# Dividing the exponentials of one block size on GpSimd instead of ScalarE, in a fused attention and two-layer expert kernel

## The chip, the cores and the metric

The kernel runs on one core of one Trainium2 chip. The metric is the time of one execution on the device in microseconds; for the kernel before there are three timed runs and one profiled execution.

## The reference, cut

Attention over 4 batches of 8 heads with 576 positions of 64 numbers, with a causal mask and a decay that comes from a running sum of log(f); then two dense layers over all 2304 tokens: one takes the largest of three products, the other puts a rational function between two products.

```
scores = scale * np.matmul(q, k.transpose(0, 1, 3, 2))
cum = np.cumsum(np.log(np.clip(f, 0.0001, 1.0)), axis=-1)
scores = np.where(causal, -1e9, scores + cum[..., :, None] - cum[..., None, :])
attn = np.exp(scores - max(scores))
attn = attn / (sum(attn) + 1e-09)          # the division that the change moves
x = np.matmul(attn, v)                      # heads side by side: 2304 x 512
h = np.maximum(np.maximum(x @ w1, x @ w2), x @ w3);  x = h @ w_out
h = x @ w_in;  out = (P(h) / (Q(h) + 1e-06)) @ w_out2
```

## The kernel before

Heads are worked on in pairs. A pair's 576 queries are split into two groups: the first has three blocks of queries (with 64, 192 and 320 keys each, by the causal mask), the second has two blocks of 128 queries, one with 448 and one with 576 keys. One head's group is a unit. In the first batch all four pairs' first groups come first (pairs 0 to 3), and then their second groups (pairs 4 to 7), so that the first dense layer can begin on the first group's columns while the second groups are still at the attention. In the three later batches a pair does both groups.

A unit goes through these steps. `scores` (L386 for the first six pairs, L388 and L389 for the others) puts queries times keys into one of two score banks in PSUM; VectorE's L390 reads the bank, adds the mask, keeps the smallest negative score and writes a block `e` to SBUF, which frees the bank; ScalarE's L396 takes exponentials and sums them. `normalise` adds a tiny number to the sums (L401, ScalarE), takes reciprocals (L402, VectorE) and multiplies each block by them: on ScalarE (L406) in the first batch's second group, on GpSimd (L408) elsewhere. `turn` transposes the blocks on TensorE (L428), and ScalarE copies them to `pt` (L430); `attend` multiplies by v (L444), and ScalarE and VectorE split the result into a high part (L451) and a low part (L452), which are `x`.

The dense layer's products in this part of the program are `h` (L476 to L478, twelve matmuls for one tile). A tile is compared with the running maximum `m` by VectorE (L484), which frees one of two banks; the products' outputs `x2p` (L502 to L504) go through L507 (ScalarE) and L508 (VectorE) to `xo`. The first `h` tile of the first batch begins with the low part of `x` of pair 3.

Beside that, weights are prepared throughout this stretch: each piece goes through L181 (ScalarE, size), L186, L187, L188 and L191 (VectorE, bit work in SBUF), L197 (ScalarE, high part) and L200 (GpSimd, low part). Keys and queries of a pair are split by L312 and L324 (ScalarE), L313 and L325 (VectorE), L314 and L328 (GpSimd).

The order of each engine's instructions is not written out by hand here: the program is recorded in steps, and a scheduler that estimates times orders it before the kernel is built. Moving one instruction to another engine therefore moves others too. Each engine then takes its instructions in that order.

Of the kernel before, what the change touches and what calls it, by code (L numbers as in the profile page):

```python
# [37 lines left out]
def kernel(  # L38
# [317 lines left out]
    class Unit:  # L356
# [41 lines left out]
        def normalise(self):  # L398
            blks = GBLK[self.g]
            n = len(blks)  # L400
            nc.scalar.activation(self.rs[:, 0, :n], self.rs[:, 0, :n], AF.Identity, bias=tiny)  # L401
            nc.vector.reciprocal(self.rs[:, 1, :n], self.rs[:, 0, :n])  # L402
            for j, i in enumerate(blks):
                e = self.e[i]
                if self.pair.b == 0 and self.g == 1:
                    nc.scalar.activation(e, e, AF.Copy, scale=self.rs[:, 1, j : j + 1])  # L406
                else:
                    nc.gpsimd.tensor_scalar(e, e, self.rs[:, 1, j : j + 1], 0.0, op0=ALU.mult, op1=ALU.add)  # L408
# [450 lines left out]
```

## Time and profile before

| what | value |
|---|---|
| median of 3 runs (lowest to highest) | 954.58 us (954.29 to 955.71) |
| profiled execution: its time | 954.83 us |
| profiled execution: its span | 953.0 us |
| TensorE busy | 932.1 us (98%) |
| VectorE busy | 723.2 us (76%) |
| ScalarE busy | 649.0 us (68%) |
| GpSimd busy | 239.7 us (25%) |

The span is the time between the first and the last instruction on the core; the profiled execution's own time has 1.8 us more around it. TensorE is busy almost throughout, so the other engines' shares say little by themselves: what counts are the few microseconds in which TensorE waits, and stretches in which its clock is at the lower of two levels.

### The profile page before, as it was taken

The numbers are of one execution on the slowest core, as the hardware profiler recorded it, in microseconds if no ns is written. First come the engines' busy times: TensorE is split into PE (matmuls) and PEld (weight loads), VectorE is DVE, ScalarE is ACT, GpSimd is POOL, SyncE is SP. The second block draws the span as 40 slices with busy tenths as digits, with TensorE's granted clock in tenths as the row PEclk, the third lists the DMA queues.
The fourth block names the chain that finished last, engine by engine and source line by source line (L and its number), as shares of the span: only waits on it lengthen the run. The fifth ranks groups of instructions, "written<-read, shape, count | busy, mean of one in ns | idle before, by whom it ended". The sixth has DMA issues, their size and how long they took to land.

```text
span 953.0 us, 16820 instructions
## 1 busy us (share of the span) xinstructions
PE 932.1 (98%) x5780; PEld 825.9 (87%) x5780; DVE 723.2 (76%) x1692; ACT 649.0 (68%) x1542; POOL 239.7 (25%) x392
## 2 busy tenths in 40 slices
PE   6999999999999999999999999999999999999998
PEld 4768899988999999999999988888888888899997
DVE  8578865556777776524397969888988988899996
ACT  6798777777777677546354567667666666777765
POOL 4344444444555455414132400000000000000000
PEclk9988999999999999999999999999999999999999
DMA  7864332123555564220245386011002102100000
GB/s 192 218 191 119 98 84 58 44 77 107 154 148 167 153 174 140 75 78 2 72 140 188 122 300 231 1 45 45 0 1 67 45 1 67 44 1 1 34 1 34
DMA packets 125743, 88.53 MB, mean 93 GB/s; under 512 B 74573, under 2 KB 110425, under 8 KB 125657
## 3 DMA queue, kind: packets, MB, share of 16 engines
q1 hardware_dynamic: 125656, 87.45, 30.6%
q8 instruction: 46, 0.75, 0.3%
q14 instruction: 41, 0.33, 0.1%
HBM read 64.73 MB, written 22.69 MB: 92 GB/s over the span
## 4 chain that ended last, share of the span: by engine, by line
PE 79%; DVE 12%; ACT 5%; issue 2%; DMA 2%; SPq 0%; ACTq 0%; DVEq 0%
PE hq L734 7%; PE oo L782 7%; PE oo L783 7%; PE hq L732 7%; PE hq L733 7%; PE oo L781 7%; PE h L476 5%; PE h L477 5%; PE h L478 5%; PE tp L428 5%; PE o L444 5%; PE s L388 2%; PE s L389 2%; PE x2p L502 2%; PE x2p L504 2%
## 5 line engine op out<-in xcount | busy, mean ns | idle before, releaser
L476 PE MATMUL h<-x,w1h 128*128 128x320 f32 (+1 forms) x576 | 175.4, 305 | 2.1 <-DVE x L452 1.3
L477 PE MATMUL h<-x,w1h 128*128 128x320 f32 (+1 forms) x576 | 171.8, 298 | 0.0
L478 PE MATMUL h<-x,w1l 128*128 128x320 f32 (+1 forms) x576 | 171.3, 298 | 0.0
L476 PEld LDWEIGHTS h<-x,w1h 128*128 128x128 f32 x576 | 109.3, 190 | 4.0 <-DVE m L484 1.9
L782 PE MATMUL oo<-wp,gh 128*128 128x512 f32 x288 | 112.6, 391 | 0.0
L781 PE MATMUL oo<-wp,gh 128*128 128x512 f32 x288 | 112.0, 389 | 0.0
L741 ACT ACTIVATE s<-hq 128x512 f32<-128x512 f32 (+1 forms) x80 | 44.3, 554 | 97.3 <-PE hq L734 97.2
L477 PEld LDWEIGHTS h<-x,w1h 128*128 128x128 f32 x576 | 109.3, 190 | 0.7 <-issue 0.5
L478 PEld LDWEIGHTS h<-x,w1l 128*128 128x128 f32 x576 | 109.1, 190 | 0.2 <-issue 0.2
L783 PE MATMUL oo<-wp,gl 128*128 128x512 f32 x288 | 109.1, 391 | 0.0
L396 ACT ACTIVATE e<-e,st 128x64 f32<-128x64 f32 (+4 forms) x160 | 88.9, 557 | 28.9 <-DVE st L390 26.5
L408 POOL TENSOR_SCALAR e<-e,rs 128x64 f32<-128x64 f32 (+4 forms) x144 | 76.2, 545 | 80.7 <-DVE rs L402 71.0
L390 DVE CUSTOM_DVE_ANT_0 e<-s,mask 128x320 f32<-128x320 f32 (+3 forms) x160 | 67.2, 432 | 32.4 <-PE s L389 21.2
L430 ACT ACTIVATE pt<-tp 128x384 f32<-128x384 f32 (+3 forms) x160 | 70.3, 469 | 15.3 <-PE tp L428 14.2
L744 DVE SCALAR_TENSOR_TENSOR s<-s,ab,u 128x512 f32<-128x512 f32 (+1 forms) x80 | 55.7, 697 | 32.2 <-ACT u L742 32.0
L428 PE MATMUL tp<-ident,e 128*128 128x128 f32 (+1 forms) x480 | 77.0, 279 | 0.0
L734 PE MATMUL hq<-x,wil 128*128 128x512 f32 (+1 forms) x192 | 69.8, 364 | 0.0
L732 PE MATMUL hq<-x,wih 128*128 128x512 f32 (+1 forms) x192 | 69.8, 363 | 0.0
L733 PE MATMUL hq<-x,wih 128*128 128x512 f32 (+1 forms) x192 | 69.6, 363 | 0.0
L783 PEld LDWEIGHTS oo<-wp,gl 128*128 128x128 f32 x288 | 54.1, 188 | 11.3
L782 PEld LDWEIGHTS oo<-wp,gh 128*128 128x128 f32 x288 | 54.0, 188 | 10.6
L781 PEld LDWEIGHTS oo<-wp,gh 128*128 128x128 f32 x288 | 54.1, 188 | 10.4
(133 smaller groups left out, 2433.7 us busy)
## 6 DMA issues: line engine op xcount, KB each, us to landing
raw_w<-in_moe_w_dram SPq DMA_DIRECT2D x18, 512.0 KB
raw_wp<-in_moe_w_out_dram SPq DMA_DIRECT2D x32, 256.0 KB
wpd<-wp SPq DMA_DIRECT2D x32, 256.0 KB
raw_wi<-in_moe_w_in_dram SPq DMA_DIRECT2D x32, 256.0 KB
wp<-wpd SPq DMA_DIRECT2D x10, 768.0 KB
x2d<-xo SPq DMA_DIRECT2D x16, 320.0 KB
out_dram<-ob SPq DMA_DIRECT2D x18, 256.0 KB
kn<-in_k_dram SPq DMA_DIRECT2D x32, 128.0 KB
```

Source lines behind the costliest of these rows:

```text
L396: nc.scalar.activation(e[:nr], e[:nr], AF.Exp, bias=m, scale=-1.0, accum_out=l)
L408: nc.gpsimd.tensor_scalar(e, e, self.rs[:, 1, j : j + 1], 0.0, op0=ALU.mult, op1=ALU.add)
L428: nc.tensor.transpose(tp[:kr, dst : dst + P], self.e[i][:, Q0[c] : Q1[c]], ident)
L476: nc.tensor.matmul(hp_[:, :w], wh[:, j, dc], xs[dc][:, 1], start=(dc == NDC - 1), stop=False)
L477: nc.tensor.matmul(hp_[:, :w], wh[:, j, dc], xs[dc][:, 0], start=False, stop=False)
L478: nc.tensor.matmul(hp_[:, :w], wl[:, j, dc], xs[dc][:, 0], start=False, stop=(dc == 0))
L732: nc.tensor.matmul(hp_[:, :w], wih[:, dc, fs], xh, start=(dc == 0), stop=False)
L733: nc.tensor.matmul(hp_[:, :w], wih[:, dc, fs], xl, start=False, stop=False)
L734: nc.tensor.matmul(hp_[:, :w], wil[:, dc, fs], xh, start=False, stop=(dc == NDC - 1))
L781: nc.tensor.matmul(o, g[0][:, ts_], wh_, start=(fc == 0), stop=False)
L782: nc.tensor.matmul(o, g[0][:, ts_], wl_, start=False, stop=False)
L783: nc.tensor.matmul(o, g[1][:, ts_], wh_, start=False, stop=(fc == NF2 - 1))
```

## The change

In the first batch's second group, the block with 448 keys (`j` is 0) is divided by GpSimd, and only the block with 576 keys (`j` is 1) stays on ScalarE.

```
             for j, i in enumerate(blks):
                 e = self.e[i]
-                if self.pair.b == 0 and self.g == 1:
+                if self.pair.b == 0 and (self.g, j) == (1, 1):
                     nc.scalar.activation(e, e, AF.Copy, scale=self.rs[:, 1, j : j + 1])
                 else:
                     nc.gpsimd.tensor_scalar(e, e, self.rs[:, 1, j : j + 1], 0.0, op0=ALU.mult, op1=ALU.add)
```

Eight units have such a block, so eight instructions change engine, and the scheduler makes another order between the first of them and the end of the first batch's attention. In the names below, the first number behind `e`, `s` and `tp` (4 to 7) or the first pair of numbers is the pair and the head, `rs` the sums and reciprocals of a unit, `cv_w` a weight piece in work, `w1l` its low part; the last number is the tile's own.

GpSimd, from the low part of the weight pieces 3 on, before:

```order
L200 TENSOR_TENSOR w1l_739<-cv_w_3_740,w1h_738 128x512
L200 TENSOR_TENSOR w1l_739<-cv_w_3_757,w1h_738 128x512
L200 TENSOR_TENSOR w1l_739<-cv_w_3_783,w1h_738 128x512
L200 TENSOR_TENSOR w1l_821<-cv_w_4_822,w1h_820 128x512
L200 TENSOR_TENSOR w1l_821<-cv_w_4_845,w1h_820 128x512
L200 TENSOR_TENSOR w1l_821<-cv_w_4_884,w1h_820 128x512
```

and after:

```order
L200 TENSOR_TENSOR w1l_739<-cv_w_3_740,w1h_738 128x512
L408 TENSOR_SCALAR e_4_0_1_813<-e_4_0_1_813,rs_0_1_812 128x448
L200 TENSOR_TENSOR w1l_739<-cv_w_3_757,w1h_738 128x512
L200 TENSOR_TENSOR w1l_739<-cv_w_3_783,w1h_738 128x512
L408 TENSOR_SCALAR e_4_1_1_918<-e_4_1_1_918,rs_1_1_917 128x448
L200 TENSOR_TENSOR w1l_821<-cv_w_4_822,w1h_820 128x512
L408 TENSOR_SCALAR e_5_0_1_1021<-e_5_0_1_1021,rs_0_1_1020 128x448
L200 TENSOR_TENSOR w1l_821<-cv_w_4_845,w1h_820 128x512
L408 TENSOR_SCALAR e_5_1_1_1141<-e_5_1_1_1141,rs_1_1_1140 128x448
```

The divisions of pairs 4 and 5 are queued between the low parts of the weight pieces.

VectorE, where pair 3's `x` is split (`x_1_0_873`, L452) and the scores of pair 5's second head are drained (L390):

```order
 L191 SCALAR_TENSOR_TENSOR cv_w_4_822<-raw_w_4_755,cv_w_4_822 128x512
 L188 SCALAR_TENSOR_TENSOR cv_w_4_845<-raw_w_4_781,cv_w_4_845 128x512
+L390 ISA e_5_1_1_1141,st_1_1_1139<-s_0_5_1_1_1142,mask 128x448
+L390 ISA st_1_1_1139 128x1
 L191 SCALAR_TENSOR_TENSOR cv_w_4_845<-raw_w_4_781,cv_w_4_845 128x512
 L452 TENSOR_TENSOR x_1_0_873<-o_1_0_864,x_1_0_873 128x320
-L390 ISA e_5_1_1_1141,st_1_1_1139<-s_0_5_1_1_1142,mask 128x448
```

The drain of the 448 scores now stands in front of the last bit operation on a weight piece and of the split of `x`.

TensorE, at the first tile of the dense layer (`h_0_0_0_892`), which follows the transposes of pair 4's second head:

```order
 L428 MATMUL tp_4_1_1_992<-ident,e_4_1_1_935 128x128 x2
 L428 MATMUL tp_4_1_1_997<-ident,e_4_1_1_935 64x128
+L386 MATMUL s_1_5_1_1_1160<-kf_119,qf_123 128x256
 L476 MATMUL h_0_0_0_892<-x_1_0_873,w1h_173 128x320
 L477 MATMUL h_0_0_0_892<-x_1_0_873,w1h_173 128x320
```

The last scores of pair 5 now stand in front of the first `h`; before, they stood two tiles later. Further on, the scores of pair 7's first head move from in front of the `h` tile 1915 to behind it, and on ScalarE L406 on 128x448 is gone from all eight units. On SyncE only one load of keys and one store of `x2d` change places.

## Rows read from the trace of the kernel before

**Rows 1.** Page, busy time of each engine over the span.

```profile
PE 932.1 (98%) x5780; PEld 825.9 (87%) x5780; DVE 723.2 (76%) x1692; ACT 649.0 (68%) x1542; POOL 239.7 (25%) x392
```

**Rows 2.** Busy time by stretch: stretch, length, each engine's busy time, granted clock, DMA.

```profile
60.00:66.40 6.40, 4.58 (x24) 2.11 (x23) 6.40 (x15) 6.30 (x17) 2.81 (x3) 1.00 0.61 189
...
66.40:76.70 10.30, 9.80 (x30) 6.60 (x31) 9.88 (x23) 9.89 (x22) 3.35 (x3) 0.50 0.70 222
...
76.70:80.10 3.40, 3.40 (x24) 3.25 (x23) 1.29 (x4) 3.40 (x10) 1.76 (x2) 1.00 0.01 2
...
77.00:146.00 69.00, 67.09 (x482) 60.69 (x482) 54.63 (x149) 54.39 (x145) 33.66 (x47) 1.00 0.34 90
```

**Rows 3.** TensorE in order of time: start, length, operation [idle before, releaser].

```profile
72.71 1.44 PE L386 MATMUL s<-kf,qf 66*128 66x320 f32 x2 [0.44 <-DVE st L390]
73.94 2.13 PE L428 MATMUL tp<-ident,e 128*128 128x128 f32 x9
75.72 0.62 PE L476 MATMUL h<-x,w1h 128*128 128x320 f32 x1
...
79.76 0.60 PE L386 MATMUL s<-kf,qf 66*128 66x256 f32 x2
```

**Rows 4.** VectorE in order of time, same columns.

```profile
66.14 0.41 DVE L187 TENSOR_SCALAR cv_w<-cv_w 128x512 int32<-128x512 int32 x1
66.59 1.64 DVE L188 SCALAR_TENSOR_TENSOR cv_w<-raw_w,cv_w 128x512 int32<-128x512 int32 x1
68.27 0.69 DVE L191 SCALAR_TENSOR_TENSOR cv_w<-raw_w,cv_w 128x512 int32<-128x512 int32 x1
...
70.17 1.09 DVE L187 TENSOR_SCALAR cv_w<-cv_w 128x512 int32<-128x512 int32 x1
...
71.51 0.15 DVE L402 RECIPROCAL rs<-rs 128x2 f32<-128x2 f32 x1
...
74.84 0.48 DVE L452 TENSOR_TENSOR x<-o,x 128x320 fp32r<-128x320 f32 x1
75.25 0.62 DVE L390 CUSTOM_DVE_ANT_0 e<-s,mask 128x448 f32<-128x448 f32 x1
```

**Rows 5.** GpSimd in order of time, same columns.

```profile
66.19 1.50 POOL L200 TENSOR_TENSOR w1l<-cv_w,w1h 128x512 fp32r<-128x512 f32 x1 [0.71 <-ACT w1h L197]
69.70 1.27 POOL L200 TENSOR_TENSOR w1l<-cv_w,w1h 128x512 fp32r<-128x512 f32 x1 [2.02 <-ACT w1h L197]
75.91 2.55 POOL L200 TENSOR_TENSOR w1l<-cv_w,w1h 128x512 fp32r<-128x512 f32 x2 [4.94 <-ACT w1h L197]
```

**Rows 6.** Groups by shape (GpSimd 150 to 480 us, ScalarE 60 to 146): busy, mean ns.

```profile
L408 POOL TENSOR_SCALAR e<-e,rs 128x448 f32<-128x448 f32 x24 | 15.8, 657 | 21.1 <-DVE rs L402 16.3 <-ACT hh L488 2.6 <-DVE st L390 1.4
...
L406 ACT ACTIVATE e<-e,rs 128x448 f32<-128x448 f32 x8 | 5.3, 667 | 0.3 <-DVE rs L402 0.2
```

**Rows 7.** ScalarE in order of time.

```profile
66.01 1.33 ACT L406 ACTIVATE e<-e,rs 128x448 f32<-128x448 f32 x2
...
72.90 1.34 ACT L406 ACTIVATE e<-e,rs 128x448 f32<-128x448 f32 x2
...
75.22 1.14 ACT L197 ACTIVATE w1h<-cv_w 128x512 fp32r<-128x512 f32 x2
...
131.64 0.67 ACT L406 ACTIVATE e<-e,rs 128x448 f32<-128x448 f32 x1 [0.23 <-DVE rs L402]
...
134.00 0.74 ACT L507 ACTIVATE xo<-x2p 128x320 fp32r<-128x320 f32 x2
```

**Rows 8.** TensorE's waits, 77 to 147 us: in total, times, longest.

```profile
PE h L476 <- DVE m L484: 0.8, 3, 0.4
PE s L388 <- DVE q1s L325: 0.4, 1, 0.4
PE x2p L502 <- DVE xo L508: 0.3, 1, 0.3
PE s L388 <- DVE st L390: 0.2, 1, 0.2
```

More of the change, by code (lines that the diff above doesn't have):

```diff
@@ L404, in normalise @@
                 e = self.e[i]
-                if self.pair.b == 0 and self.g == 1:
+                if self.pair.b == 0 and (self.g, j) == (1, 1):
                     nc.scalar.activation(e, e, AF.Copy, scale=self.rs[:, 1, j : j + 1])
```

## The prediction, made before the changed kernel was run

> **What bounds the kernel now.** I read the page first, then the busy time by stretches, then each engine in time order from 62 to 80 us, and last the waits of TensorE behind that. The page has TensorE (PE) busy for 932.1 of 953.0 us [rows 1], so a gain must come out of the 21 us in which it stands still, or out of time in which it runs at the lower clock. An engine beside it that is merely relieved gives nothing. The instructions that the change moves lie between 66 and about 135 us; behind that every engine's order is as before; what the stretch from 66 to 146 us gains or loses is handed on one for one.
>
> In that stretch there are two regimes. From 66.4 to 76.7 us the granted clock is 0.50 throughout, that is 1.2 GHz, against 1.00 in the 3.4 us behind it [rows 2]. TensorE was busy for 4.58 of the 6.40 us ahead of the fall [rows 2], and it has only scores (L386) and transposes (L428) during it, until the dense h products start at 75.72 [rows 3]. VectorE (DVE) and ScalarE (ACT) are busy for 9.88 and 9.89 of these 10.3 us [rows 2]. Here TensorE's pace hangs on VectorE: a score bank is free only once L390 has drained it. The row at 72.71 shows it, 0.44 us idle released by L390 [rows 3]. VectorE fills the time between drains with the bit work on the expert weights (L186 to L191). From 77 us on there is so much product work that TensorE stands still for only 69.00 - 67.09 = 1.91 us up to 146 [rows 2], in short waits, all listed ones for VectorE [rows 8].
>
> **The parts of the change.** *The division itself.* The first batch has eight second-group units. Each loses one ScalarE instruction on 128x448, 667 ns, and gains a GpSimd one on the same block, 657 ns [rows 6]. Eight times 0.667 are 5.3 us off ScalarE. The two blocks of a unit were divided one behind the other, 1.33 us for the pair [rows 7]; they can now run side by side, so the transposes of either may be ready some 0.6 us sooner. No transpose is listed as waiting for ScalarE here [rows 3, 8], so the 0.6 us are worth nothing by themselves.
>
> *What the GpSimd instruction does to VectorE.* The trace shows a price on the other side. L187 on 128x512 takes 0.41 us alone at 66.14, but 1.09 us at 70.17, where it began while GpSimd's L200 (69.70 to 70.97) was running [rows 4, 5]. L188 at 66.59 takes 1.64 us, and ends 0.54 us behind the L200 that began at 66.19 and ended at 67.69, whereas the like-shaped L191 at 68.27 takes 0.69 [rows 4, 5]. So bit work that starts inside a GpSimd instruction waits for its end. Until now GpSimd had nothing but L200 here. The Trainium skill says the same more sharply (SBUF — State Buffer, "Who interferes with whom"): the port pair that the two engines share is locked for a whole instruction, and the second one blocks fully; by that rule the new divisions can only cost VectorE time, and the time saved on ScalarE doesn't offset it.
>
> *66 to 77 us, step by step.* (a) The first division needs the same reciprocal as the ScalarE pair that starts at 66.01 [rows 7]; it begins there or a little sooner and lasts 0.66 us, to about 66.5. L187 at 66.14 then starts inside it, and ends some 0.3 us late. L200, L188 and L191 move by the same 0.3 and don't add to it. Bounds: 0 (it slips into the L390 ahead) and 0.66. (b) The second division comes right behind the reciprocal at 71.51 [rows 4], in front of L186 and L188. Bounds 0 and 0.66; I take the middle, 0.35, since it depends on which of them starts first. (c) The L200 that was at 75.91, beside the drains [rows 5], now starts about half a microsecond sooner, since ScalarE reaches the L197 ahead of it (75.22, [rows 7]) without the division of 0.67 us at 72.90. Its 1.3 us then lie on L191, which is now behind a drain (the order above). Bounds 0 and 0.96, the most that a bit operation was held up (1.64 - 0.68); I take 0.5. (d) The drain of 0.62 us at 75.25 now stands ahead of the subtraction L452, which makes the low half of x that the first h product reads: 0.62 us, certain. L452 ended at 74.84 + 0.48 = 75.32. In sum it ends at 75.32 + 0.3 + 0.35 + 0.5 + 0.62 = 77.1 us, and h starts there and not at 75.72: 1.4 us late. Of this 0.6 us are no loss, because the scores that ran at 79.76 for 0.60 us [rows 3] now run in front of h. Net **+0.8 us**.
>
> The low end: with no hold-up L452 ends at 75.94 and h starts behind the scores moved forward, at 76.3: no loss. Below nothing: the h products that ran at half clock from 75.72 to 76.68 would run at full clock if the clock rises as before and they come later, 0.5 us at best. So -0.5. The high end: 0.66 + 0.66 + 0.96 + 0.62 on 75.32 are 78.2, less 75.72 and 0.6: +1.9.
>
> *77 to 146 us.* The other six divisions lie beside dense products. Two of TensorE's waits should go. One of 0.4 us for q1s [rows 8]: the scores of unit 7 now stand behind twelve more products (some 2 us). One of 0.3 us for xo [rows 8]: ScalarE reaches L507 at 134.0 without the division at 131.64 (0.67, [rows 7]). Against that, six GpSimd instructions of 0.66 us can hold up bit work ahead of L484, which frees the h banks; these waits are 0.8 us in three [rows 8]. Six times half of 0.66 would be 2 us of VectorE, which is busy for 54.63 of the 69.00 us [rows 2], so most of it goes into its idle time; I take 0.2. Together **-0.5 us**. Bounds: -1.9, when all waits of the stretch vanish; upwards 2 us, when all of that VectorE time reaches TensorE.
>
> GpSimd's other work (L200, L490, L314, L328) changes places among itself by a few rows at most, and no DMA is added. SyncE's swap of a key load with a store of x2d has no waiter among TensorE's waits, so nothing.
>
> **Sum.** The profiled execution took 954.83 us, 953.0 of span and 1.8 around it; the median of the three runs is 954.58, 0.25 below. 954.83 + 0.8 - 0.5 = 955.1, and against the median 954.9. I say **955.0 us**. About 0.2% (1.9 us) is what a measurement of this kernel tells from no change, so this counts as no change.
>
> **Rivals.** *The low clock lasts longer (slower).* In before, h had been running for 0.96 us when the clock rose at 76.7; in after it starts at about 77.1, and the time ahead of it holds only the sparse scores and transposes that went on at half clock from 66.4 on [rows 2, 3]. If the rise needs the dense products, it slips with them. Another stretch as long as the one from 76.7 to 80.1 (3.4 us, dense, [rows 2]) at half clock does half its work: +1.7 us on top of the +0.3, 956.8. A slip by just the 1.4 us of h's lateness costs 0.7: 955.8. It decides by whether h has begun by 76.7: lateness above 1 us, so the bounds above straddle it. For it: at 0.50 the trace shows nothing but sparse work until h. Against it: only 0.5 us of idle time are in the whole stretch [rows 2], and VectorE's hold-ups may be at their low ends. The Trainium skill (TensorE: Matmul & The Clock Gate, "What's actually happening") states that the lower rate is the default and that activity releases it; by that rule the rise follows h, and the trace agrees as far as one rise shows it. Chance 0.27.
>
> *ScalarE was the true limit (faster).* It is busy for 9.89 of 10.3 us [rows 2] and gets 1.3 us less to do there; if VectorE's row of work was held by ScalarE's pace, TensorE's waits in 66.4 to 76.7 (0.50) and 77 to 146 (1.91) [rows 2] go together: 954.83 - 2.4 = 952.4. Against it: VectorE's rows show no idle time from 66 to 75.8 [rows 4], and the waits name VectorE [rows 8]. Chance 0.12.
>
> *GpSimd's queue (slower).* A division can stand behind an L200 that waits for ScalarE's L197, and the transposes behind the division. L200 takes 1.3 us [rows 5]; two such waits that reach TensorE are 2.6 us, 957.7. Against it: the L200 ahead of the second division ended at 70.97 [rows 5], before the reciprocal at 71.51 [rows 4] that the division needs as well. Chance 0.06.
>
> That the change does nothing is excluded: ScalarE's order has eight rows fewer and GpSimd's eight more.
>
> **How the numbers follow.** Forecast 0.55, long low clock 0.27, ScalarE 0.12, GpSimd's queue 0.06. The forecast's own bounds are -0.5 to +1.9 and -1.9 to +2 about 954.6, mostly inside 953.4 to 956.4. The range takes in the long low clock at 956.8 with some lateness on top, and leaves out the far ends of the ScalarE and queue cases: 953.2 to 957.3. Faster by over 0.2% (below 952.7) needs nearly the whole ScalarE case: 0.11. Slower by over 0.2% (above 956.5) is the long low clock, the queue, and none of the 0.7 us slip: 0.29. Same: 0.60.
>
> **What would show it.** In the profile after: L187 and L188 near 66 to 68 us and the bit work near 72 us longer where a GpSimd L408 overlaps them; L452 of the first x at 76.5 to 77.7 and h right behind it; the clock at 0.50 again from 66.4, its end either at 76.7 (forecast) or some 3 us later (rival). In 77 to 146 the wait for xo gone, and TensorE idle for 1.2 to 2 us. I am wrong if h starts before 76.3, if the half clock is shorter than 10 us, or if a transpose is seen waiting for GpSimd.

## The result, and the profile after

The changed kernel takes 960.35 us (median of six runs, 959.30 to 961.21), the kernel before 955.47 us in the runs beside it: ratio 1.0052, 95% interval 1.0040 to 1.0063. That is 4.9 us slower, beyond the 0.2% that can be told from no change, and outside the range of 953.2 to 957.3.

The profiled execution took 960.80 us, 5.97 above that of before. The page's row of busy times, beside [rows 1]:

```profile
PE 936.2 (98%) x5780; PEld 828.8 (86%) x5780; DVE 726.6 (76%) x1692; ACT 646.1 (67%) x1534; POOL 245.0 (26%) x400
```

ScalarE is busy for 2.9 us less, GpSimd for 5.3 more. TensorE is busy for 4.1 us longer with the same instructions, so part of the loss is slower work and not waiting. Stretches of TensorE (stretch, length, busy, granted clock, DMA share, GB/s), which answer to [rows 2]:

```profile
65.40:82.50 17.10, 15.66 (x46) 0.50 0.51 158
...
77.00:146.00 69.00, 65.70 (x446) 0.96 0.30 80
...
125.00:151.00 26.00, 24.04 (x178) 1.00 0.32 86
```

The half clock lasts 17.1 us and not 10.3. From 77 to 146 us TensorE stands still for 3.3 us and not 1.9. TensorE in order of time, beside [rows 3] (start, length, operation [idle before, releaser]):

```profile
73.34 0.69 PE L428 MATMUL tp<-ident,e 128*128 128x128 f32 x2 [0.46 <-POOL e L408]
...
74.89 1.70 PE L428 MATMUL tp<-ident,e 128*64 128x128 f32 x7
76.57 1.22 PE L386 MATMUL s<-kf,qf 66*128 66x256 f32 x2
78.23 0.63 PE L476 MATMUL h<-x,w1h 128*128 128x320 f32 x1 [0.44 <-DVE x L452]
...
82.40 0.36 PE L476 MATMUL h<-x,w1h 128*128 128x320 f32 x1
```

A transpose waits 0.46 us for a GpSimd division, and the first h product starts at 78.23, 2.5 us later than in before. VectorE and GpSimd say why, beside [rows 4, 5]:

```profile
66.46 0.71 DVE L187 TENSOR_SCALAR cv_w<-cv_w 128x512 int32<-128x512 int32 x1
...
71.86 0.40 DVE L186 TENSOR_SCALAR cv_w<-cv_w 128x512 f32<-128x512 f32 x1
72.19 0.68 DVE L188 SCALAR_TENSOR_TENSOR cv_w<-raw_w,cv_w 128x512 int32<-128x512 int32 x1
...
74.13 0.68 DVE L188 SCALAR_TENSOR_TENSOR cv_w<-raw_w,cv_w 128x512 int32<-128x512 int32 x1
75.89 0.62 DVE L390 CUSTOM_DVE_ANT_0 e<-s,mask 128x448 f32<-128x448 f32 x1 [1.08 <-PE tp L428]
...
76.44 1.34 DVE L191 SCALAR_TENSOR_TENSOR cv_w<-raw_w,cv_w 128x512 int32<-128x512 int32 x1
77.70 0.48 DVE L452 TENSOR_TENSOR x<-o,x 128x320 fp32r<-128x320 f32 x1
```

```profile
66.25 0.64 POOL L408 TENSOR_SCALAR e<-e,rs 128x448 f32<-128x448 f32 x1 [0.46 <-DVE rs L402]
...
72.04 1.25 POOL L408 TENSOR_SCALAR e<-e,rs 128x448 f32<-128x448 f32 x1 [0.46 <-DVE rs L402]
75.96 1.27 POOL L200 TENSOR_TENSOR w1l<-cv_w,w1h 128x512 fp32r<-128x512 f32 x1 [2.67 <-ACT w1h L197]
```

The drain at 75.89 is the one that the new order put ahead of L452. It stood idle for 1.08 us until transposes had ended. It fills block 3 of pair 5, head 1, and that block lies in the buffer of block 3 of pair 4, head 1, which those transposes were still reading. L191 and L452 queue behind it. In before they stood ahead of the drain and filled that time. Less the shift of 0.31 us explained below, L452 starts 2.55 us later than in before: 0.30 come from the stretched L187 at 66.46, 1.08 from the drain's wait, 0.55 from the drain itself and 0.65 from L191, which runs beside the L200 at 75.96.

Where the 5.97 us arise can be read by the start of like instructions in both traces. At the last attend of pair 3 (61 us, order still common) the changed run is already 0.31 us late, in work that the change doesn't touch. That shift is taken off in what follows. At a product of pair 4's attend (L444, 81.41 us in before) it is 3.26 us late, at pair 9's first key transpose (151.05 us in before) 5.11. From there on it is handed on nearly one for one: 5.7 at the first product of the last stage (L732, 553.9 us in before).

So there are two places. **First, 66 to 82 us: 3.26.** h starts 2.20 us late (77.92 less shift, against 75.72), 0.60 of it regained by the scores moved ahead: 1.6. And h then runs at half clock from 78.23 to 82.4, 4.2 us, where before it did so for 1.0 us: half of the 3.2 us, 1.6. **Second, 82 to 151 us: 1.85**. Between the two points TensorE stands still for 3.1 us and not 1.9; the other 0.7 us lie in time that counts as busy. All listed waits of TensorE from 77 to 147 us (in total, times, longest), beside [rows 8]:

```profile
PE tk L335 <- ACT pt L430: 1.1, 2, 0.8
PE x2p L502 <- DVE xo L508: 1.0, 1, 1.0
PE x2p L502 <- ACT wo L197: 0.5, 1, 0.5
PE h L476 <- DVE x L452: 0.4, 1, 0.4
```

### The profile page after: what moved, and what is told of

It is laid out like the page before. It is cut to its first block, busy times and chain, and to the rows that moved or that the text cites. A ratio compares the mean times of both kernels' runs of the same rounds, so it can differ in the third digit from the quotient of the medians.

```text
span 959.0 us, 16831 instructions
## 1 busy us (share of the span) xinstructions
PE 936.2 (98%) x5780; PEld 828.8 (86%) x5780; DVE 726.6 (76%) x1692; ACT 646.1 (67%) x1534; POOL 245.0 (26%) x400
## 4 chain that ended last, share of the span: by engine, by line
PE 85%; DVE 7%; ACT 3%; issue 2%; DMA 2%; SPq 1%; POOL 0%; ACTq 0%; DVEq 0%
PE hq L734 7%; PE hq L732 7%; PE oo L783 7%; PE oo L782 7%; PE hq L733 7%; PE h L476 7%; PE oo L781 7%; PE h L477 7%; PE h L478 7%; PE o L444 5%; PE tp L428 5%; PE s L388 2%; PE s L389 2%; PE x2p L502 2%; PE x2p L504 2%; PE x2p L503 2%
## 5 line engine op out<-in xcount | busy, mean ns | idle before, releaser
L408 POOL TENSOR_SCALAR e<-e,rs 128x64 f32<-128x64 f32 (+4 forms) x152 | 82.8, 560 | 90.4 <-DVE rs L402 78.2
L390 DVE CUSTOM_DVE_ANT_0 e<-s,mask 128x320 f32<-128x320 f32 (+3 forms) x160 | 67.1, 431 | 33.5 <-PE s L389 21.0
L430 ACT ACTIVATE pt<-tp 128x384 f32<-128x384 f32 (+3 forms) x160 | 69.8, 469 | 13.7 <-PE tp L428 12.7
L732 PE MATMUL hq<-x,wih 128*128 128x512 f32 (+1 forms) x192 | 69.8, 363 | 0.0
L484 DVE TENSOR_TENSOR m<-m,h 128x320 f32<-128x320 f32 (+1 forms) x96 | 43.1, 449 | 26.7 <-PE h L478 14.1
L782 PEld LDWEIGHTS oo<-wp,gh 128*128 128x128 f32 x288 | 54.0, 188 | 10.5
```

The lines of the kernel that those rows point to most:

```text
L732: nc.tensor.matmul(hp_[:, :w], wih[:, dc, fs], xh, start=(dc == 0), stop=False)
L782: nc.tensor.matmul(o, g[0][:, ts_], wl_, start=False, stop=False)
```

## Experiments

Each kernel was timed against the kernel before on the same chip. The table is read as above: start of the first h less the shift at 61 us, length of the half-clock spell around it, lateness against before at the two points, and the ratio of the times.

| run | first h | half clock, us | late at 81 us | late at 151 us | ratio (95% interval) |
|---|---|---|---|---|---|
| before | 75.72 | 10.3 | 0 | 0 | 1 |
| changed | 77.92 | 17.1 | 3.26 | 5.11 | 1.0052 (1.0040 to 1.0063) |
| e1 | 77.94 | 17.1 | 3.48 | 3.93 | 1.0044 (1.0031 to 1.0058) |
| e2 | 75.78 | 13.7 | 1.20 | 1.10 | 1.0013 (1.0001 to 1.0024) |
| e3 | 77.38 | 13.7 | 2.34 | 4.66 | 1.0051 (1.0031 to 1.0071) |
| e4 | 75.74 | 10.2 | 0.46 | 0.38 | 0.9997 (0.9987 to 1.0008) |
| e5 | 75.94 | 10.2 | -0.02 | 3.47 | 1.0031 (1.0017 to 1.0046) |
| e6 | 75.72 | 6.8 | 0.27 | 6.97 | 1.0078 (1.0051 to 1.0104) |
| e7 | 75.72 | 10.3 | 0.53 | 0.57 | 1.0005 (0.9996 to 1.0015) |
| e8 | 77.93 | 10.2 | 1.36 | 3.16 | 1.0041 (1.0026 to 1.0057) |
| e9 | 76.58 | 10.3 | 0.58 | 4.25 | 1.0042 (1.0027 to 1.0057) |
| e10 | 75.89 | 3.4 | -0.26 | -0.09 | 1.0026 (1.0014 to 1.0037) |
| e11 | 75.88 | 10.3 | -0.42 | 4.29 | 1.0039 (1.0026 to 1.0052) |
| e12 | 76.17 | 10.3 | -0.98 | 4.70 | 1.0048 (1.0033 to 1.0063) |
| e13 | 77.94 | 17.0 | 3.63 | 5.12 | 1.0052 (1.0033 to 1.0072) |
| e14 | 75.51 | 6.9 | 4.59 | 1.27 | 1.0020 (1.0008 to 1.0032) |

In e5, e6, e11 and e12 the last scores of pair 5 (0.6 us) come only behind the first point, and in e11 and e12 some h products too, so their lateness there looks too favourable. In e14, 24 h products that stood behind the first point come ahead of it, and in e9 eleven that stood behind the second come ahead of that; there part of the lateness is moved work. e1 and e13, whose order up to 82 us is that of the changed kernel, have its long half clock as well (17.1 and 17.0 us), so it isn't one execution's.

The median has what one trace doesn't: runs of one kernel differ. Among the 23 runs of before beside e1 to e4, the eleven with a mean clock of 0.995 took 954.39 to 957.41 us and the four at 0.991 and 0.989 took 956.94 to 958.16, but the eight between them 953.61 to 957.14, so the mean clock goes with only part of that spread. The runs of the changed kernel have 0.989 to 0.993.

### One place or two: e1, e2

e1 keeps the GpSimd division in pairs 4 and 5 alone, e2 in pairs 5, 6 and 7:

```diff
-                if self.pair.b == 0 and (self.g, j) == (1, 1):
+                if self.pair.b == 0 and self.g == 1 and (j == 1 or self.pair.n in (6, 7)):      # e1
+                if self.pair.b == 0 and self.g == 1 and (j == 1 or self.pair.n not in (5, 6, 7)):  # e2
```

> Only the four units of pairs 4 and 5 divide their 448-key block on GpSimd; the units of pairs 6 and 7 divide it on ScalarE as before. Every engine's order is that of the changed kernel up to about 130 us. Theory (two places of loss: the late first h with the long low clock, and hold-ups at 112 to 146 us): h starts near 78 us, the low clock ends near 82.5, and the loss of the second place (2 to 2.5 us) is gone: before + 3.2, about 958.5. Rival A (only the first place counts, the loss behind 112 us is its echo): before + 5.5, about 960.5. Rival B (only the later divisions cost, the first delay is made good): before + 0 to 0.5.

> The units of pairs 5, 6 and 7 divide on GpSimd, the two of pair 4 on ScalarE as before. With that VectorE's order from 66 to 78 us is that of before, L452 ahead of the drain. Theory of two places: the first h starts within 0.5 us of before's 75.7, the low clock ends near 76.7, and only the loss at 112 to 146 us stays: before + 2 to 2.5, about 957.5. Rival A (one place): before + 0 to 0.5, about 955.5. Rival B (only the later divisions cost): before + 5, about 960.

Measured: e1 959.96 us, e2 957.00, before 956.03. e1 has all of the first place (3.48) and is 3.9 us slower; from 82 to 151 us, without the late divisions, it loses only 0.45. e2, with six of the eight divisions and L452 ahead of the drain as in before, starts h on time. The first place makes most of the loss, and it goes with pair 4. Two things in e2 fit none of the three. It keeps four divisions from 82 to 151 us and loses nothing there (1.20 to 1.10), so the second place isn't a price per division. And its clock stayed at half for 13.7 us, 3.6 of them behind the start of h, though h started on time once its shift at 61 us (2.36) is taken off; that alone is its 1.2 us at the first point (TensorE in order of time, then the half-clock stretch):

```profile
78.14 0.61 PE L476 MATMUL h<-x,w1h 128*128 128x320 f32 x1
```

```profile
68.00:81.70 13.70, 12.62 (x39) 0.50 0.58 185
```

### Which division of pair 4: e3, e4

Both leave one more division on ScalarE: e3 that of pair 4, head 1 (near 72 us), e4 that of head 0 (near 66 us); the lists go on with all units of pairs 5 to 7.

```diff
-                if self.pair.b == 0 and (self.g, j) == (1, 1):
+                if self.pair.b == 0 and self.g == 1 and (j == 1 or (self.pair.n, self.h) not in [(4, 0), (5, 0), ...]):  # e3
+                if self.pair.b == 0 and self.g == 1 and (j == 1 or (self.pair.n, self.h) not in [(4, 1), (5, 0), ...]):  # e4
```

> As the changed kernel, but head 1 of pair 4 divides on ScalarE: no GpSimd division beside VectorE's bit work at 72 us. The drain of pair 5 still stands ahead of L452 (here directly ahead of it, behind L191). Theory that the order makes the lateness: the drain waits for pair 4's last transposes, h starts 1.2 to 2 us later than before (77 to 77.7), the low clock lasts beyond 79 us, and the time is within 1 us of the changed kernel's, before + 4 to 5. Rival (the hold-ups by GpSimd make it): the drain's wait is under 0.5 us, h starts at about 76.5, the clock rises by 78, before + 2 to 2.5.

> As the changed kernel, but head 0 of pair 4 divides on ScalarE: the division at 72 us stays on GpSimd beside VectorE's bit work, and L452 stands ahead of the drain as before. Theory that the order makes the lateness: the GpSimd division is again stretched to about 1.2 us and transposes wait 0.3 to 0.5 us for it, but h starts at 75.7 to 76.3 and the low clock ends at 76.7 to 77.5: before + 2 to 2.5. Rival (the hold-ups make it): h starts at 77 or later, low clock beyond 79 us, before + 4 to 5.

Measured: e3 960.77 us, e4 955.75, before 956.03. This is the sharpest pair: seven divisions each. e3, VectorE in order of time:

```profile
74.77 0.69 DVE L191 SCALAR_TENSOR_TENSOR cv_w<-raw_w,cv_w 128x512 int32<-128x512 int32 x1
76.26 0.62 DVE L390 CUSTOM_DVE_ANT_0 e<-s,mask 128x448 f32<-128x448 f32 x1 [0.80 <-PE tp L428]
...
76.81 0.49 DVE L452 TENSOR_TENSOR x<-o,x 128x320 fp32r<-128x320 f32 x1
```

No GpSimd division is near, and the drain ahead of L452 waits all the same, 0.80 us. In e4 the division is there, and costs nothing; TensorE, GpSimd, VectorE:

```profile
72.77 0.69 PE L428 MATMUL tp<-ident,e 128*128 128x128 f32 x2 [0.54 <-POOL e L408]
...
75.67 0.61 PE L476 MATMUL h<-x,w1h 128*128 128x320 f32 x1
...
71.71 1.00 POOL L408 TENSOR_SCALAR e<-e,rs 128x448 f32<-128x448 f32 x1 [0.79 <-DVE rs L402]
...
74.83 0.48 DVE L452 TENSOR_TENSOR x<-o,x 128x320 fp32r<-128x320 f32 x1
75.32 0.62 DVE L390 CUSTOM_DVE_ANT_0 e<-s,mask 128x448 f32<-128x448 f32 x1
```

The division is stretched to 1.00 us and a transpose waits 0.54 us for it, more than in the changed kernel, and yet L452 is at 74.83 and h at 75.67. The order makes most of the lateness: e3 keeps 1.66 of the 2.20 us with no division near. In e3 L191 stands ahead of the drain and isn't stretched (0.69 us against 1.34), which fits the rest.

### Holding the order by hand: e5, e6

e5 is the changed kernel, e6 the one before, each with L452 of pair 3 and the drain of pair 5, head 1, kept in program order.

```diff
-                nc.vector.tensor_tensor_reduce(
+                (pinned if (p.n, h, n) == (5, 1, 0) else lambda ins: ins)(nc.vector.tensor_tensor_reduce(
...
-            nc.vector.tensor_tensor(x[:, 1], ot[:, :w], r32(x[:, 0]), op=ALU.subtract)
+            (pinned if p.n == 3 else lambda ins: ins)(nc.vector.tensor_tensor(x[:, 1], ...))
```

> The changed kernel with all eight GpSimd divisions, and one thing held: the subtraction L452 of the fourth x and the drain L390 of block 3 of pair 5, head 1, keep their order in the program, so that L452 stands ahead of that drain as in before. The scheduler moves other instructions behind it too. Theory from e3 and e4 (the drain ahead of L452 makes the loss, not the divisions): h starts at 75.5 to 76.5 us and the time is before + 0 to 1. Rival (eight divisions cost by themselves, e4 was spared since it has one less): h at 76.5 or later and before + 2.5 or more.

> The kernel before (all divisions on ScalarE) with the same two instructions held in program order as in e5: what the holding does by itself, since the drain then lies further behind L452 than in before. Theory: h at 75.7 as in before; before + 0 to 0.5. Rival (the holding shifts the later order as much as the change does): before + 1.5 to 4. If this and e5 agree within 1 us, the divisions cost nothing by themselves.

Measured: e5 958.74, e6 964.06, before 955.75. As times the two say little: the hold pushed the scores of block 4 of pair 5 some 18 us back, and that costs the kernel before 8 us by itself. What can be read is the first place: with all eight divisions and L452 ahead of the drain, h starts at 75.94 and nothing is late at 81 us (-0.02, or +0.6 with the scores still to come).

### The late divisions alone: e7

Only the two units of pair 7 divide on GpSimd (the condition as in e2, with `(7,)`).

> Only the two units of pair 7 divide on GpSimd; VectorE's order is that of before in every row, TensorE's differs in 18 of 4000 rows. What the late divisions cost where the order stays. Theory of e2 and e4 (no cost by themselves): before + 0 to 0.5, TensorE idle in 125 to 151 us within 0.5 us of before's 0.5. Rival (the hold-ups of VectorE's bit work at 131 to 136 us, seen in the changed kernel, come with the GpSimd instruction): 1 to 2 us of idle time more there, before + 1 to 2.

Measured: 956.60 against 955.75, no difference that can be told. Lateness at 151 us is 0.57, of which 0.53 were there at 81 us, ahead of its first GpSimd division. In before's order these two divisions cost nothing.

### What the clock costs: e8

```diff
-            for _ in range(WARM):
+            for _ in range(2 if n == 0.5 else WARM):
...
-                sp = exercised(ps_s.tile(...), p.n)
+                sp = exercised(ps_s.tile(...), 0.5 if (self.nm, i, n) in [('5_1_1', 3, 0), ('5_1_1', 4, 1)] else p.n)
```

(with `if n < 4` unchanged, 0.5 switches the warm products on for these two banks)

> The changed kernel with four more warm products (128x512, results unused, as the kernel has them in its first four pairs): two ahead of the scores of block 3 and two ahead of the last scores of block 4 of pair 5, head 1, just before the first h. VectorE's, ScalarE's and GpSimd's orders are those of the changed kernel. At half clock they add some 1.7 us to TensorE, of which about 1.5 us lie in its idle time of 70 to 78 us. Theory (the clock comes back after dense work, so it comes sooner when that starts sooner): low clock ends 1 to 3 us earlier, at 79.5 to 81.5, and the changed kernel - 0.5 to - 1.5. Rival (the rise doesn't depend on it): low clock still ends near 82.5, the changed kernel + 0 to 1.

Measured: 959.58 us, ratio 1.0041. VectorE and TensorE in order of time, then the half-clock stretch:

```profile
75.94 0.62 DVE L390 CUSTOM_DVE_ANT_0 e<-s,mask 128x448 f32<-128x448 f32 x1 [1.21 <-PE tp L428]
...
76.63 1.22 PE L84 MATMUL s<-warm 128*128 128x512 f32 x2
...
78.16 0.41 PE L476 MATMUL h<-x,w1h 128*128 128x320 f32 x1
78.41 0.30 PE L477 MATMUL h<-x,w1h 128*128 128x320 f32 x1
```

```profile
67.70:77.90 10.20, 8.87 (x26) 0.50 0.64 210
```

The drain waits as before and h starts at the same point (77.93 against 77.92 less shift), but the clock is up at 77.9, ahead of h, and the products take 0.30 us and not 0.47. At 81 us the run is 1.36 us late and not 3.26: **the long half clock is worth 1.9 us in these traces**, the late start 1.4. The spell also began 2.3 us later here; how much of its shortness each pair of warm products made can't be told. Between the medians, from different sets of runs, 0.8 us of gain is left, and the intervals overlap.

### The drain without its wait: e9

```diff
-            self.e[i] = apool.tile([P, keys], F32, name=f"e{i}_{self.nm}", tag=f"e{i}_{h}")
+            own = (self.nm, i) == ("5_1_1", 3); self.e[i] = apool.tile([P, NB * 2 * D if own else keys], F32, name=f"e{i}_{self.nm}", tag="vs" if own else f"e{i}_{h}", bufs=3 if own else 1)[:, :keys]
```

> The changed kernel, with block 3 of pair 5, head 1, in a buffer of its own (one that a v tile of an earlier pair has left) and no longer in the one that it shares with pair 4, head 1. The drain L390 that fills it still stands ahead of L452, but need not wait for pair 4's last transposes; one L191 slips behind L452, and the order differs further on. Theory (the lateness of h is mostly this wait): VectorE's 1.1 us of idle time ahead of that drain is gone, h starts at 75.7 to 76.7 us, the low clock ends before 79, before + 0 to 1.5. Rival (the drain's own 0.6 us and the hold-ups make it): idle time ahead of the drain 0.7 us or more, h at 77 or later, before + 3 to 5.

Measured: 959.62 us, ratio 1.0042. VectorE, then TensorE:

```profile
73.81 0.61 DVE L390 CUSTOM_DVE_ANT_0 e<-s,mask 128x448 f32<-128x448 f32 x1
...
74.95 0.48 DVE L452 TENSOR_TENSOR x<-o,x 128x320 fp32r<-128x320 f32 x1
...
76.56 0.83 PE L476 MATMUL h<-x,w1h 128*128 128x320 f32 x1
```

In its own buffer the drain stands ahead of L452 and no longer waits; L452 is back at 74.95, h waits only for the scores ahead of it in TensorE's queue, the half clock ends at 77.6, and the lateness at 81 us is 0.58. That is the first place as the theory has it, but the wait is not all that went: L191 also slipped behind L452, so its 1.34 us no longer hold up L452. The time isn't as expected: the order changed further on, and at the first product of the last stage the run is 3.3 us late.

### Other ways to the old order: e10, e11, e12

e10 is the changed kernel with warm products ahead of the transposes of pair 4, head 1, which happen to bring L452 ahead of the drain; e11 divides the 576-key block on GpSimd and the 448-key one on ScalarE; e12 divides both on GpSimd.

```diff
-            tp = exercised(ps_t.tile(...), self.pair.n)
+            tp = exercised(ps_t.tile(...), 0 if self.nm == "4_1_1" else self.pair.n)   # e10
-                if self.pair.b == 0 and (self.g, j) == (1, 1):
+                if self.pair.b == 0 and (self.g, j) == (1, 0):   # e11
+                if self.pair.n < 0:                              # e12
```

> The changed kernel with all eight divisions on GpSimd, plus two warm products (128x512, results unused) ahead of each of the three banks of transposes of pair 4, head 1. They make the scheduler put L452 ahead of the drain of pair 5 again, as in before, without holding anything. Theory (order, not divisions): h at 75.7 to 76.7 us, low clock over by 78, and with up to 1.5 us of added products on TensorE's way before + 0 to 1.5. Rival (eight divisions cost by themselves): before + 3 or more.

> GpSimd divides the 576-key block of the eight units and ScalarE the 448-key one: the longer instruction on GpSimd. The scheduler then puts L452 ahead of the drain and of the last two bit operations. Theory (what counts is where L452 and the drain stand): h at 75 to 76.2 us, no longer low clock, before - 0.5 to + 1. Rival (the GpSimd instruction is the price, and it is a third longer): more than the changed kernel's + 5.

> GpSimd divides both blocks in all eight units, sixteen divisions, ScalarE none. L452 stands ahead of the drains that follow it. Theory: the same as for the swap, with some 0.5 us for transposes that wait for the second division of a unit (about 1.5 us for the two on GpSimd): before + 0 to 1.5. Rival (price per GpSimd instruction): twice the changed kernel's, before + 8 to 10.

Measured: 957.53, 958.74 and 960.05 us, before 955.33. All three start h within 0.5 us of before, none has the long half clock, and e10, with all eight divisions, is at 151 us where before is (-0.09). Its median is 2.2 us above before all the same. In its trace that arises in one place, just ahead of the last stage, where it is 1.5 us late: ScalarE stands idle ahead of an L507 until a store of `x2d` has ended, 4.61 us where before has 2.46, and TensorE waits for the `xo` behind it (ScalarE, then a row of TensorE's waits from 545 to 575 us):

```profile
554.75 0.38 ACT L507 ACTIVATE xo<-x2p 128x256 fp32r<-128x256 f32 x1 [4.61 <-DMA x2d<-xo]
```

```profile
PE hq L732 <- DVE xo L508: 1.6, 1, 1.6
```

e8 and e14 have the same wait (1.2 and 0.9 us), before and the changed kernel don't; why the store ends late stays open. e11 and e12 miss: they lose 4.7 and 5.7 us from 82 to 151 us by the table, in part work that moved. It isn't a price per instruction (e12 has twice the divisions of the changed kernel and the same time), but I did not find which of their moved rows it is.

### The second place: e13

```diff
+                if self.pair.b == 0 and self.g == 1 and (j == 1 or self.nm in ['7_0_1']):
```

> The changed kernel, but head 0 of pair 7 divides both its blocks on ScalarE; orders are those of the changed kernel, but for two rows that change places on VectorE and some six on TensorE. Theory A (the hold-ups by that GpSimd division make the wait for xo at 140 us): bit operations at 131 to 135 us take 0.4 us and no longer 0.8 to 1.1, the wait for xo falls below 0.3 us, TensorE's idle time in 125 to 151 us falls from 2.0 to about 1 us, and the time by 0.8 to 1.2 us: before + 3.5 to 4.2. Theory B (the order makes it, with the weights' bit work late in VectorE's queue and ScalarE waiting for it): the wait for xo stays at 0.7 us or more, before + 4.5 to 5.2.

Measured: 961.30 us, ratio 1.0052, lateness at 151 us 5.12 as in the changed kernel, the wait for xo still 1.0 us: theory B. From 82 to 151 us it loses 1.5 us where the changed kernel loses 1.85, so a third of a microsecond at most is the division's. In the changed kernel the chain reads so (VectorE, ScalarE, VectorE, TensorE):

```profile
132.79 1.10 DVE L191 SCALAR_TENSOR_TENSOR cv_wo<-raw_wo,cv_wo 128x256 int32<-128x256 int32 x1
...
133.93 0.42 ACT L197 ACTIVATE wo<-cv_wo 128x256 fp32r<-128x256 f32 x1 [1.69 <-DVE cv_wo L191]
...
139.42 0.75 ACT L507 ACTIVATE xo<-x2p 128x320 fp32r<-128x320 f32 x2
139.88 0.89 DVE L508 TENSOR_TENSOR xo<-x2p,xo 128x320 fp32r<-128x320 f32 x2 [1.94 <-ACT xo L507]
...
140.42 0.42 PE L502 MATMUL x2p<-hh,wo 128*128 128x320 f32 x1 [0.96 <-DVE xo L508]
```

The bit work on the last weights holds ScalarE's queue, and L507 behind it comes late. Without the division at 131.7 us the wait stays. In e13, a row of TensorE's waits from 125 to 151 us, and VectorE and GpSimd in order of time:

```profile
PE x2p L502 <- DVE xo L508: 1.0, 1, 1.0
```

```profile
131.56 0.88 DVE L188 SCALAR_TENSOR_TENSOR cv_wo<-raw_wo,cv_wo 128x256 int32<-128x256 int32 x1
132.36 0.97 DVE L187 TENSOR_SCALAR cv_wo<-cv_wo 128x256 int32<-128x256 int32 x1
...
132.12 1.05 POOL L490 TENSOR_TENSOR hh<-m,hh 128x320 fp32r<-128x320 f32 x1
```

GpSimd's next instruction, L490, took the division's place beside the bit work and holds it up in the same way, so e13 took away a division and not the hold-up. But hold-ups alone don't make the loss: the 48 bit operations on these weights add up to 21.1 us in before, 22.8 in the changed kernel, and 23.3 in e4 and 22.4 in e10, which lose at most 0.2 us from 82 to 151. What differs from the kernels without the wait is when that bit work comes at all. ScalarE's L197 on the last weights from 110 to 138 us (count, ns, first to last start), in before, then in e4, then in the changed kernel:

```profile
L197 ACT ACTIVATE wo<-cv_wo x8: 404/417/422, 112.0 to 129.5; 128x256 fp32r<-128x256 f32 x8
```

```profile
L197 ACT ACTIVATE wo<-cv_wo x7: 403/416/418, 113.3 to 129.9; 128x256 fp32r<-128x256 f32 x7
```

```profile
L197 ACT ACTIVATE wo<-cv_wo x9: 400/409/418, 112.1 to 136.1; 128x256 fp32r<-128x256 f32 x9
```

The last of them starts 6.6 us later in the changed kernel than in before; counted from the first product of pair 4's attend it is 52.3 us and not 49.3. In e1, e2, e4, e7 and e10, which lose less than 0.5 us from 82 to 151, it is 48.9 to 50.0 us; in e3, e8, e9, e11, e12 and e13, which lose 1.5 or more by the table, 51.6 to 54.3. (e5 and e6 lose time elsewhere: TensorE waits 1.5 and 2.7 us for q2s.) e1, e2 and e4, of which the last two have the same late divisions, have no such wait for xo above 0.2 us. So the second place needs the two together: the late divisions cost at most 0.2 us in the orders of e2, e4 and e10, and the changed kernel's order up to some 130 us costs 0.45 us without them (e1). Whether the late divisions then act by holding up bit work or by the order that they bring with them isn't shown; no run moved the weights' bit work alone.

### Does the half clock cost the kernel before: e14

```diff
-            tp = exercised(ps_t.tile(...), self.pair.n)
+            tp = exercised(ps_t.tile(...), 0 if self.nm == "4_0_1" else self.pair.n)
```

> The kernel before, with two warm products (128x512, results unused) ahead of each of the three banks of transposes of pair 4, head 0, at 66 to 70 us. Theory: the clock stays up some microseconds longer and the low spell of 10.2 us gets shorter, by 3 us or more; scores and transposes wait for VectorE there anyway, so only what lies on TensorE's way is gained: before - 1 to + 0.5. Rival (the added products, 1.3 us at full clock, lie on TensorE's way or move the later order): before + 1 or more.

Measured: 958.10 us against 956.70, ratio 1.0020. The spell got shorter (6.9 us), but the later order changed, and 1.27 us are lost at 151 us. No gain, and no version here beats the kernel before; e4 equals it.

## Why the prediction was wrong

*The sum:* +0.8 and -0.5, so +0.3 us, against 5.11 at 151 us. Of the 4.8 between them 0.8 are the lateness of h (1.6 net and not 0.8), some 1.6 the half clock in h, which the forecast had at nothing and left to a rival, and some 2.4 the stretch from 82 us on.

*The division itself, and that ScalarE's relief is worth nothing:* right. ScalarE lost 2.9 us and TensorE gained none.

*(a) and (b), hold-ups of VectorE by the two divisions:* (a) right, L187 took 0.71 us in place of 0.41. (b) the wrong way round: VectorE's L186 had started first, it and the L188 behind it kept their 0.40 and 0.68 us, and the division took 1.25 us. L188 began at 72.19 inside the division (from 72.04) and did not wait, so "bit work that starts inside a GpSimd instruction waits for its end" doesn't always hold. A transpose then waited 0.46 us, the sign that I had named for being wrong. e4 has (b) and no loss; e5 and e10 have both, in before's order of L452 and the drain, and start h 0.2 us late.

*(c) L200 on L191:* right, 1.34 us in place of 0.69, so 0.65 where I took 0.5.

*(d) "The drain of 0.62 us at 75.25 now stands ahead of the subtraction L452 ... 0.62 us, certain":* **this is the step that failed first.** I charged the drain with its own length and took VectorE's row of work as full, since it showed no idle time in before. But the drain writes a buffer that pair 4's transposes still read, and in before L191 and L452 filled the time until then. Moved ahead of them it waits, 1.08 us (0.80 in e3, none in e9, where it has a buffer of its own). The sum had L452 end at 77.1; it ended at 77.9 less shift, the wait added and the 0.35 us of (b) not there. The buffer tag, which pair 5 shares with pair 4, stood in the code; I asked which engine runs the moved instruction and not whose data it overwrites.

*Rival "the low clock lasts longer", 0.27:* it is what happened, and its condition held, lateness above 1 us with h not begun by 76.7. Its price for the clock, 1.7 us, was near what was measured: half of the 3.2 us that h ran longer at half clock, 1.6, and 1.9 by e8, with the clock up 4.6 us sooner behind the four added products and h at the same place. That is luck in part: the 3.4 us came from a stretch picked in the rows, and no row of before says that a longer spell lasts that long. Its 956.8 was too low because it kept the forecast's other two terms, h late by 1.4 us (2.2 less shift) and -0.5 behind 77 us. The Trainium skill's rule quoted there (TensorE: Matmul & The Clock Gate, "What's actually happening"), that activity releases the lower rate, agrees with e8 and e9 (up at 77.9 us behind added products, and at 77.6, 1.0 us into h). e2 qualifies it: h on time and dense, yet 3.6 us at half clock before the rise (1.0 in before), so a start in time made the early rise likely and not certain.

*77 to 146 us, -0.5:* the largest single miss, some 2.4 us, since 1.85 were lost from 82 to 151. The wait for q1s went, as forecast; that for xo grew from 0.3 to 1.0, and two waits for ScalarE came. I looked at the divisions there one by one and found their cover, which e7 and e4 confirm in their own orders; I didn't price the rearranged weights' bit work around them.

*That the stretch's loss is handed on one for one:* nearly right, 5.11 at 151 us and 5.7 at the first product of the last stage. *Rivals ScalarE and GpSimd's queue:* neither; no L408 stood behind a waiting L200.

## What to carry over

When a scheduler moves an instruction ahead of one on the critical path, price it by what it waits for at its new place, and look first at the buffer that it writes: who read that buffer last, and when does that reader end? A small edit under a scheduler is two edits, the work that moved and the order that moved with it, and here the first had hardly any price without the second; e3 and e4 show how to test them apart. A stall ahead of the first dense work after a sparse stretch may cost twice, once as time and once more as clock.

## What was not expected of the hardware

A GpSimd instruction that starts inside VectorE's bit work is the one that is stretched: 1.25 us and not 0.64 at 72.04, while L188 behind it kept 0.68 us; in the other order L187 took 0.71 us at 66.46 in place of 0.41. The Trainium skill says so (SBUF — State Buffer, "Who interferes with whom": issue order decides who blocks). L186 (71.86, ahead of the division) and L187 (66.46, behind one that began at 66.25) agree with it; L188 doesn't, which began 0.15 us behind the division and went ahead of it.

The half-clock spell in the same part of the program lasted from 3.4 us (e10) to 17.1 (changed), and another, somewhere from 14 to 24 us, came in eight of the sixteen traces only, with the same instructions in the same order; in the changed run, with TensorE busy throughout (stretch, length, busy, granted clock, DMA share, GB/s):

```profile
17.60:21.00 3.40, 3.40 (x12) 0.51 0.53 116
```

In e2 it lasted about twice as long, and that run was 2.36 us late at 61 us; the changed run was 0.31 late there, but e13, without such a spell, 0.40. How much of the 4 us or so by which executions of one kernel differ comes from it is not shown.
